# A state-space scan and its squared-ReLU network on one core: small products gathered in one region per block, other PSUM banks, DMA transposes, other weight packets

## The chip, the core and the metric

The kernel runs on one core of a Trainium2 chip. TensorE (PE) multiplies: a weight load puts a stationary block into its array, a matmul streams another operand through it, and the result lands in PSUM, which has eight banks of 512 fp32 columns on 128 partitions. VectorE (DVE) and ScalarE (ACT) read PSUM and work on SBUF; GpSimd (POOL) works on SBUF alone; SyncE (SP) and ACT issue DMAs. Each engine runs its own instructions in order and waits on semaphores for the others.

The metric is the device time in microseconds. Each time below is a median over executions; lower is better.

## The reference

A chunked scan (chunks of 32 tokens in the reference; the kernel is free to choose) for 4 batches, 8 heads, 768 tokens, head size 32 and state size 16, then a two-layer network on the 3072 tokens.

```python
L = exp(cum[i] - cum[j]) * causal            # decay between tokens of a chunk
y = einsum(C_i, B_j) * L @ x                 # within the chunk
y += einsum(C, state) * exp(cum)             # from the state before the chunk
state = exp(sum(la)) * state + sum_j B_j x_j * exp(cum_last - cum_j)
...
h = maximum(Y @ w_in, 0)                     # Y: 3072 x 256, w_in: 256 x 2048
out = (h * h) @ w_out                        # w_out: 2048 x 256
```

## The kernel before

**Units and blocks.** The 3072 tokens are 12 units of 256: unit k is (batch b, third j) in the order of `PAIRS`, all batches of the first third, then of the second, then of the last. A unit is two chunks of 128 tokens (`u` = 0, 1); its tokens are split in even and odd (`r`). The scan of unit k gives a 256 x 256 tile `T[k]`, and block k of the network takes it. The decay is folded in by products: C is multiplied by the running product P of `a`, x by its inverse, and the state by the product over a chunk (`Ptot`).

**A unit's steps** (functions of the same names):
- `ph_load`: three DMAs for C, B and x. `ph_prep` (POOL): scaled C into a zeroed tile `cz`, B cast to `Bb`, scaled x into `xs`.
- `ph_tr`: six PE transposes of 128x128 into PSUM, then one DVE copy to `bct`.
- `ph_u`: 16 matmuls (64x32 weights) for the new part of the state, then DVE: `z` = U + state, S = z times Ptot, twice in a row.
- `ph_mt`: 16 matmuls (32x64 weights) of C with B, over four banks. `ph_mask` (DVE): four times 512 columns times the causal mask, into `mts`.
- `ph_y`: up to 16 matmuls with 32x32 weights from the state and 32 from `mts` and `xs`; ACT copies the result to `T`.

**A block of the network** is 8 steps. Step (blk, fp): `mm1` has four matmuls of 128x128 weights and 256 columns into one bank and ACT's ReLU; `square` on DVE; `mm2` four more into a bank that is kept over the block. After the last, ACT copies it to `osb` and SP stores it. In a step only the four large matmuls of mm1 and of mm2, 0.44 us each, are on PE.

**Order.** It is written out by hand: `with tc.manual_schedule()` (line 329), the loads, the first two units complete, and then a loop over 96 steps: mm1 of step s, what `todo` holds for s, the square of s-1, mm2 of s-4. A unit's pieces stand at five different steps (lines 393 to 404), each between two fours of large matmuls. The PSUM pools give two banks to mm1, two to mm2, four to the pieces of the scan.

**Weights.** Five pairs of DMAs (`load_w`), on ACT's and SP's queue, bring them as fp32, w_in in columns and w_out in rows of 1 KB; `cast_w` makes them bf16, w_in on ACT and w_out on POOL, in five pieces.

Of the kernel before, what the change touches and what calls it, by code (L numbers as in the profile page):

```python
# [30 lines left out]
def kernel(  # L31
# [13 lines left out]

    nc = tc.nc
    NH, S, D, N = 8, 768, 32, 16
    NPAIR = 12
    LAG = 4
    LEAD = 12  # L50
# [6 lines left out]
    big = ctx.enter_context(tc.tile_pool(name="big", bufs=2))  # L57
# [5 lines left out]
    ps_h = ctx.enter_context(tc.tile_pool(name="ps_h", bufs=2, space=bass.MemoryType.PSUM))  # L63
    ps_o = ctx.enter_context(tc.tile_pool(name="ps_o", bufs=2, space=bass.MemoryType.PSUM))
    ps_s = ctx.enter_context(tc.tile_pool(name="ps_s", bufs=1, space=bass.MemoryType.PSUM))


    tok = 2 * np.arange(64)[None, :] + np.arange(2)[:, None]
    later = tok.reshape(-1)
    mask_np = np.zeros((128, 2, 128), np.float32)  # L70
    for u in range(2):
        for r in range(2):
            mask_np[64 * u:64 * u + 64, r, :] = (tok[r][:, None] <= later[None, :])
# [6 lines left out]
    cb_np = np.concatenate([np.eye(128, dtype=np.float32), mask_np.reshape(128, 256)],  # L80
                           axis=1).astype(ml_dtypes.bfloat16)
# [4 lines left out]
    cb = const.tile([128, 384], BF16, name="cb")  # L86
# [13 lines left out]
    cz = [const.tile([128, 2, 240], BF16, name=f"cz{i}") for i in range(3)]  # L100
# [6 lines left out]
    PAIRS = [(b, j) for j in range(3) for b in range(4)]  # L107


    loaded = {}  # L110

    def ph_load(k, order="CBx", eng=None):
        b, j = PAIRS[k]
        t = {}
        for what in order:
            src, w = {"B": (B, N), "C": (C, N), "x": (x, D)}[what]
            dst = nat.tile([128, NH, 2 * w], FP32, tag=f"{what}_nat", name=f"{what}_nat{k}")
            (eng or nc.sync).dma_start(  # L118
                out=dst, in_=_dap(src, (b * NH * S + j * 256) * w,
                                  [[2 * w, 128], [S * w, NH], [1, 2 * w]]))  # L120
            t[what] = dst
        loaded[k] = t

    def load_w(f0, f1, eng):
        eng.dma_start(  # L125
            out=w_in_f[:, :, f0 * 128:f1 * 128],
            in_=_dap(moe_w_in, f0 * 128, [[2048, 128], [128 * 2048, 2], [1, (f1 - f0) * 128]]))
        eng.dma_start(  # L128
            out=w_out_f[:, f0:f1, :],
            in_=moe_w_out[f0 * 128:f1 * 128, :].rearrange("(f p) d -> p f d", p=128))  # L130

    def cast_w(f0, f1):
        nc.scalar.copy(out=w_in_b[:, :, f0 * 128:f1 * 128], in_=w_in_f[:, :, f0 * 128:f1 * 128])  # L133
        nc.gpsimd.tensor_copy(out=w_out_b[:, f0:f1, :], in_=w_out_f[:, f0:f1, :])  # L134

# [3 lines left out]
    def prep_c(k, eng):  # L139
        b, j = PAIRS[k]  # L140
        czk = cz[k % 3]
        eng.tensor_tensor(  # L142
            out=_fap(czk, 0, [[240, 2], [32, 8], [1, 16]]),
            in0=_fap(loaded[k]["C"], 0, [[16, 2], [32, 8], [1, 16]]),
            in1=_fap(P_sb, b * 24 + j, [[96, 2], [3, 8], [0, 16]]), op=ALU.mult)
        live.setdefault(k, {})["cz"] = czk

    def prep_b(k, eng):
        Bb = prep.tile([128, 2, 128], BF16, tag="Bb", name=f"Bb{k}")
        for r in range(2):  # L150
            bo = _fap(Bb, r * 128, [[16, 2], [32, 4], [1, 16]])
            bi = _fap(loaded[k]["B"], r * 16, [[128, 2], [32, 4], [1, 16]])
            if eng is nc.scalar:
                eng.copy(out=bo, in_=bi)  # L154
            else:
                eng.tensor_copy(out=bo, in_=bi)  # L156
        live.setdefault(k, {})["Bb"] = Bb

    def prep_x(k, eng):
        b, j = PAIRS[k]  # L160
# [14 lines left out]
    def ph_tr(k):  # L175
        v = live[k]
        pool, tag = (ps_o, "ops") if k < 2 else (ps_s, "A")
        tr = pool.tile([128, 2, 3, 128], BF16, tag=tag, name=f"tr{k}",
                       padded_shape=[128, 2, 4, 128] if k < 2 else [128, 8, 4, 128])
        for r in range(2):  # L180
            nc.tensor.transpose(tr[:, r, 0, :], v["Bb"][:, r, :], eye_b)  # L181
            for g in range(2):
                nc.tensor.transpose(tr[:, r, 1 + g, :], v["cz"][:, r, 112 * g:112 * g + 128], eye_b)  # L183
        bct = big.tile([128, 2, 3, 128], BF16, tag="bct", name=f"bct{k}")
        nc.vector.tensor_copy(out=bct, in_=tr)  # L185
        v["bct"] = bct

    def ph_mt(k):
        v = live[k]
        bct = v["bct"]  # L190
        mt = ps_s.tile([128, 4, 2, 2, 128], FP32, tag="A", name=f"mt{k}")
        for u in range(2):
            for r in range(2):
                for q in range(4):
                    nc.tensor.matmul(  # L195
                        mt[64 * u:64 * u + 64, q, r, :, :],
# [4 lines left out]
        v["mt"] = mt  # L201
        v["mts"] = big.tile([128, 4, 2, 2, 128], BF16, tag="mts", name=f"mts{k}")

    def ph_mask(k, q):
        v = live[k]
        nc.vector.tensor_tensor(  # L206
            out=v["mts"][:, q], in0=v["mt"][:, q],
            in1=_fap(cb, 128, [[128, 2], [0, 2], [1, 128]]), op=ALU.mult)

    def ph_u(k):  # L210
        b, j = PAIRS[k]
        v = live[k]
        if k < 2:
            U = [ps_h.tile([128, 64], FP32, tag="hps", name=f"U{k}_{u}", padded_shape=[128, 512])
                 for u in range(2)]
        else:
            t = ps_s.tile([128, 4, 512], FP32, tag="A", name=f"U{k}")
            U = [t[:, u, 0:64] for u in range(2)]
        for r in range(2):
            for u in range(2):  # L220
                if j == 2 and u == 1:
                    continue
                for q in range(4):
                    nc.tensor.matmul(  # L224
                        U[u][32 * q:32 * q + 32, :],
                        v["Bb"][64 * u:64 * u + 64, r, 32 * q:32 * q + 32],
                        _fap(v["xs"][64 * u:64 * u + 64], r * 256 + q * 32, [[128, 2], [1, 32]]),
                        start=(r == 0), stop=(r == 1), skip_group_check=True,
                        tile_position=(64 * u, 32 * q))
        S_u = [state.get(b)]  # L230
        for u in range(2):
            if j == 2 and u == 1:
                break
            ptot = Ptot[:, u, b * 3 + j:b * 3 + j + 1]
            S_n = spool.tile([128, 64], BF16, tag=f"S{b}{u}", name=f"S{k}_{u}")
            if S_u[u] is None:
                nc.vector.tensor_scalar(out=S_n, in0=U[u], scalar1=ptot, scalar2=None, op0=ALU.mult)  # L237
            else:
                z = spool.tile([128, 64], FP32, tag="z", name=f"z{k}_{u}")
                nc.vector.tensor_tensor(out=z, in0=U[u], in1=S_u[u], op=ALU.add)  # L240
                nc.vector.tensor_scalar(out=S_n, in0=z, scalar1=ptot, scalar2=None, op0=ALU.mult)
            S_u.append(S_n)
        v["S"] = S_u
        state[b] = S_u[-1]

    T = {}

    def ph_y(k):
        b, j = PAIRS[k]
        v = live.pop(k)  # L250
        if k < 2:
            Y = [ps_h.tile([128, 2, 128], FP32, tag="hps", name=f"Y{k}_{u}", padded_shape=[128, 4, 128])
                 for u in range(2)]
        else:
            t = ps_s.tile([128, 4, 4, 128], FP32, tag="A", name=f"Y{k}")
            Y = [t[:, u, 0:2, :] for u in range(2)]
        first = {(u, q): True for u in range(2) for q in range(4)}
        for u in range(2):
            S_b = v["S"][u]
            if S_b is None:  # L260
                continue
            for g in range(2):
                for q in range(4):
                    nc.tensor.matmul(  # L264
                        Y[u][32 * q:32 * q + 32, g, :],
                        S_b[32 * q:32 * q + 32, g * 32:(g + 1) * 32],
                        _fap(v["bct"][32 * q:32 * q + 32], 128 + g * 128 + u * 64, [[384, 2], [1, 64]]),
                        start=first[(u, q)], stop=False, skip_group_check=True,
                        tile_position=(32 * q, 32 * q))
                    first[(u, q)] = False  # L270
        for g in range(2):
            for r in range(2):
                for u in range(2):
                    for q in range(4):
                        h = 4 * g + q
                        nc.tensor.matmul(  # L276
                            Y[u][32 * q:32 * q + 32, g, :],
                            v["xs"][64 * u:64 * u + 64, r, h * 32:h * 32 + 32],
                            v["mts"][64 * u:64 * u + 64, q, r, g, :],
                            start=first[(u, q)], stop=(g == 1 and r == 1), skip_group_check=True,  # L280
# [163 lines left out]
```

## Time and profile before

| | us |
|---|---|
| median of 3 runs (131.95 to 132.62) | 132.33 |
| span of the profiled execution | 129.5 |
| PE busy in it | 111.8 |
| DVE busy | 90.4 |
| ACT busy | 75.7 |
| POOL busy | 31.6 |

The profiled execution's span runs from its first to its last instruction; the time of a run lies 2.83 us above it. Granted TensorE clock: 0.997. A line of the chain of waits has the start, the length and what was on the path then. In a table of windows, each engine has its busy time and, in brackets, its instructions. In a line on groups "idle before" is the time its engine sat still just before, and the arrow names what ended it. L numbers are lines of the kernel.

### The profile page before, as it was taken

The page shows a single profiled execution, that of the slowest core. Times are in us where ns is not written, and L with a number is a line of the kernel's source. Part 1 is how long each engine was busy: PE and PEld are TensorE (multiplying, and loading weights), DVE is VectorE, ACT ScalarE, POOL GpSimd, SP SyncE. Part 2 cuts the span into 40 slices and gives each one's busy share as a digit, 9 for nine tenths or more (in the row PEclk, how much of TensorE's full clock was granted, in tenths as well). Part 3 has the DMA queues.
Part 4 walks back from the last instruction along what each step waited for, and adds up shares of the span by engine and source line. Part 5 has one row for each costly group of instructions (what it writes and reads, how often), then busy time and mean ns, then how long its engine had stood idle before and what let it go on. Part 6 is the DMA issues. An engine that isn't in the chain of part 4 may idle for free.

```text
span 129.5 us, 4148 instructions
## 1 busy us (share of the span) xinstructions
PE 111.8 (86%) x1740; PEld 87.8 (68%) x1740; DVE 90.4 (70%) x201; ACT 75.7 (58%) x134; POOL 31.6 (24%) x54
## 2 busy tenths in 40 slices
PE   0126648699999999999999999999999999999980
PEld 0013315557877787788778777887887787788860
DVE  0519592379899698795896995886977938744520
ACT  0413308867757657658467476576584675687740
POOL 4015236335907025060070240330330000000000
PEclk9999999999999999999999999999999999999998
DMA  4999999978391280650831903805602010020202
GB/s 95 257 165 262 294 175 269 318 148 154 96 200 21 88 161 6 137 106 5 177 69 47 196 10 96 149 3 135 116 0 89 3 68 18 0 86 0 81 0 81
DMA packets 43043, 14.18 MB, mean 110 GB/s; under 512 B 37840, under 2 KB 40720, under 8 KB 43024
## 3 DMA queue, kind: packets, MB, share of 16 engines
q1 hardware_dynamic: 42224, 13.21, 43.8%
q10 hardware_dynamic: 800, 0.71, 1.8%
q8 instruction: 13, 0.21, 0.7%
q14 instruction: 6, 0.05, 0.1%
HBM read 10.77 MB, written 3.15 MB: 107 GB/s over the span
## 4 chain that ended last, share of the span: by engine, by line
PE 76%; SPq 11%; DMA 8%; ACT 1%; issue 1%
PE ops L321 34%; PE hps L301 30%; SPq L118 8%; DMA w_in_f<-in_moe_w_in_dram 6%; PE mt L195 3%; PE Y L276 3%; PE Y L264 2%; DMA cf<-const_f 2%; SPq L125 2%; PE tr L183 2%; PE U L224 1%; SPq L128 1%; ACT w_in_b L133 1%; PE tr L181 1%; ACT osb L326 0%
## 5 line engine op out<-in xcount | busy, mean ns | idle before, releaser
L305 ACT ACTIVATE hb<-hps 128x512 bf16<-128x512 f32 x96 | 57.5, 599 | 32.2 <-PE hps L301 31.1
L301 PE MATMUL hps<-T,w_in_b 128*128 128x256 bf16 x384 | 58.5, 277 | 1.8 <-ACT w_in_b L133 1.4
L321 PE MATMUL ops<-w_out_b,h 128*128 128x256 bf16 x384 | 57.3, 273 | 0.0
L311 DVE TENSOR_TENSOR h<-hb 128x512 bf16<-128x512 bf16 x96 | 45.9, 500 | 9.4 <-ACT hb L305 9.4
L301 PEld LDWEIGHTS <-w_in_b 128*128 128x128 bf16 x384 | 38.0, 99 | 7.6 <-ACT w_in_b L133 1.9
L321 PEld LDWEIGHTS <-h 128*128 128x128 bf16 x384 | 34.7, 98 | 7.0 <-issue 2.0
L206 DVE TENSOR_TENSOR mts<-mt,cb 128x512 bf16<-128x512 f32 x48 | 31.5, 685 | 2.8 <-PE mt L195 2.7
L162 POOL TENSOR_TENSOR xs<-x_nat,Pinv 128x512 bf16<-128x512 f32 x12 | 13.5, 1126 | 15.0 <-DMA x_nat<-in_x_dram 11.7
L142 POOL TENSOR_TENSOR cz<-C_nat,P_sb 128x256 bf16<-128x256 f32 x10 | 6.8, 682 | 40.4 <-DMA C_nat<-in_C_dram 28.8
L185 DVE COPY bct<-tr 128x768 bf16<-128x768 bf16 x12 | 6.7, 556 | 13.4 <-PE tr L183 13.4
L326 ACT COPY osb<-ops 128x512 f32<-128x512 f32 x12 | 7.0, 580 | 1.6 <-PE ops L321 1.6
L276 PE MATMUL Y<-mts,xs 64*32 64x128 bf16 x384 | 6.2, 232 | 1.8 <-DVE mts L206 1.8
L181 PE MATMUL tr<-cb,Bb 128*128 128x128 bf16 x24 | 5.1, 232 | 3.0 <-ACT Bb L154 3.0
L290 ACT CAST T<-Y 128x512 bf16<-128x512 f32 x10 | 5.9, 586 | 1.3
L195 PE MATMUL mt<-bct 32*64 32x256 bf16 x192 | 5.7, 302 | 0.7 <-DVE bct L185 0.7
L156 POOL CAST Bb<-B_nat 128x128 bf16<-128x128 f32 x20 | 5.8, 319 | 1.8 <-DMA B_nat<-in_B_dram 1.7
L264 PE MATMUL Y<-bct,S 32*32 32x128 bf16 x160 | 4.6, 225 | 1.9 <-DVE S L237 1.9
L276 PEld LDWEIGHTS <-xs 64*32 64x32 bf16 x384 | 3.4, 95 | 3.8 <-issue 1.7
L183 PE MATMUL tr<-cb,cz 128*128 128x128 bf16 x48 | 5.9, 235 | 0.0
L134 POOL CAST w_out_b<-w_out_f 128x1024 bf16<-128x1024 f32 (+1 forms) x5 | 4.3, 868 | 6.0 <-DMA w_out_f<-in_moe_w_out_dram 6.0
L264 PEld LDWEIGHTS <-S 32*32 32x32 bf16 x160 | 2.3, 91 | 4.3 <-DVE S L237 2.2
L287 ACT CAST T<-Y 128x256 bf16<-128x256 f32 x4 | 1.3, 376 | 6.5 <-PE Y L276 6.5
(29 smaller groups left out, 37.8 us busy)
## 6 DMA issues: line engine op xcount, KB each, us to landing
x_nat<-in_x_dram SPq DMA_DIRECT2D x12, 256.0 KB, 4.2
out_dram<-osb SPq DMA_DIRECT2D x12, 256.0 KB, 2.2
C_nat<-in_C_dram SPq DMA_DIRECT2D x12, 128.0 KB, 3.5
B_nat<-in_B_dram SPq DMA_DIRECT2D x12, 128.0 KB, 4.1
w_in_f<-in_moe_w_in_dram SPq DMA_DIRECT2D x3, 512.0 KB, 5.8
w_out_f<-in_moe_w_out_dram SPq DMA_DIRECT2D x3, 512.0 KB, 7.1
w_in_f<-in_moe_w_in_dram ACTq DMA_DIRECT2D x1, 256.0 KB, 4.8
w_out_f<-in_moe_w_out_dram ACTq DMA_DIRECT2D x1, 256.0 KB, 5.2
```

The source lines that it names most:

```text
L118: (eng or nc.sync).dma_start(out=dst, in_=_dap(src, (b * NH * S + j * 256) * w, [[2 * w, 128], [S * w, NH], [1, 2 * w]]))
L162: eng.tensor_tensor(out=_fap(xs, 0, [[256, 2], [32, 8], [1, 32]]), in0=_fap(loaded[k]["x"], 0, [[32, 2], [64, 8], [1, 32]]), in1=_fap(Pinv ...
L183: nc.tensor.transpose(tr[:, r, 1 + g, :], v["cz"][:, r, 112 * g:112 * g + 128], eye_b)
L195: nc.tensor.matmul(mt[64 * u:64 * u + 64, q, r, :, :], bct[32 * q:32 * q + 32, r, 0, u * 64:u * 64 + 64], _fap(bct[32 * q:32 * q + 32], 12 ...
L206: nc.vector.tensor_tensor(out=v["mts"][:, q], in0=v["mt"][:, q], in1=_fap(cb, 128, [[128, 2], [0, 2], [1, 128]]), op=ALU.mult)
L264: nc.tensor.matmul(Y[u][32 * q:32 * q + 32, g, :], S_b[32 * q:32 * q + 32, g * 32:(g + 1) * 32], _fap(v["bct"][32 * q:32 * q + 32], 128 + ...
L276: nc.tensor.matmul(Y[u][32 * q:32 * q + 32, g, :], v["xs"][64 * u:64 * u + 64, r, h * 32:h * 32 + 32], v["mts"][64 * u:64 * u + 64, q, r, ...
L301: nc.tensor.matmul(hps[:, i, :], w_in_b[:, g, f * 128:(f + 1) * 128], T[blk][:, g].rearrange("p r u t -> p (r u t)"), start=(g == 0), stop ...
L305: nc.scalar.activation(out=hb, in_=hps, func=AF.Relu)
L311: nc.vector.tensor_tensor(out=h2, in0=hb, in1=hb, op=ALU.mult)
L321: nc.tensor.matmul(ops[blk][:, r, :], h2[:, i, r * 128:(r + 1) * 128], w_out_b[:, f, :], start=(f == 0 and r == 0), stop=(f == 15), skip_g ...
L326: nc.scalar.copy(out=osb, in_=ops.pop(blk).rearrange("p r d -> p (r d)"))
```

## The change

- The transposes of units 4 to 11 are DMA transposes on SP's queue, SBUF to SBUF. B and scaled C are for this put side by side in one tile `jt` per unit (three of them, zeroed once).
- All PSUM is one tile `pp` of eight banks: 0 to 3 for `ph_mt`, 4 to 6 in turn for everything else (`bank`, `two_banks`), 7 for mm2.
- The state is also kept as a 128x256 block-diagonal tile (`S_d`), so that Y from the state is two full-array matmuls a chunk. `ph_s` has z on DVE and the two scalings on POOL.
- Y of unit k, U of unit k+1 and the products of `ph_mt` of unit k+1 stand together, once a block (`ph_yu`, then `ph_mt`). U and Y share a bank: columns 256 to 319 and 0 to 255.
- The mask is applied to two banks at a time.
- w_out is read so that a partition gets 2 or 4 neighbouring rows (2 or 4 KB); the columns of w_in are taken in the matching order when they are cast. The casts are eight pieces, two before the loop.
- Only unit 0 is complete before the loop; unit 1 is made in the first eight steps. In a step, `todo` comes before mm1. B of unit 0 is loaded from ACT's queue, all weights from SP's; the loads of later units are issued ten steps earlier.

```diff
-    ps_h = ctx.enter_context(tc.tile_pool(name="ps_h", bufs=2, space=bass.MemoryType.PSUM))
-    ps_o = ctx.enter_context(tc.tile_pool(name="ps_o", bufs=2, space=bass.MemoryType.PSUM))
-    ps_s = ctx.enter_context(tc.tile_pool(name="ps_s", bufs=1, space=bass.MemoryType.PSUM))
+    psum = ctx.enter_context(tc.tile_pool(name="psum", bufs=1, space=bass.MemoryType.PSUM))
...
+    pp = psum.tile([128, 8, 512], FP32, name="pp")
+    turn = [4]
+    def bank():
+        h = turn[0]
+        turn[0] = 4 if h == 6 else h + 1
+        return h
+    def two_banks():
+        h = turn[0] if turn[0] < 6 else 4
+        turn[0] = 6 if h == 4 else 4
+        return h, h + 1
...
-    def cast_w(f0, f1):
-        nc.scalar.copy(out=w_in_b[:, :, f0 * 128:f1 * 128], in_=w_in_f[:, :, f0 * 128:f1 * 128])
-        nc.gpsimd.tensor_copy(out=w_out_b[:, f0:f1, :], in_=w_out_f[:, f0:f1, :])
+    def cast_w(fp):
+        f = 2 * fp
+        f0, f1 = next(x for x in BLOCKS if x[0] <= f < x[1])
+        nc.scalar.copy(out=_fap(w_in_b, f * 128, [[2048, 2], [128, 2], [1, 128]]),
+                       in_=_fap(w_in_f, f0 * 128 + f - f0, [[2048, 2], [1, 2], [f1 - f0, 128]]))
+        nc.gpsimd.tensor_copy(out=w_out_b[:, f:f + 2, :], in_=w_out_f[:, f:f + 2, :])
...
     def ph_tr(k):
+        if k >= NPE:
+            nc.sync.dma_start_transpose(out=bct.rearrange("p r w t -> p (r w) t"),
+                                        in_=jt[k % 3].rearrange("p r w t -> p (r w t)"))
+            return
...
+    def ph_mask(k, q0, q1):
+        nc.vector.tensor_tensor(
+            out=live[k]["mts"][:, q0:q1].rearrange("p q r g i -> p q (r g i)"), in0=pp[:, q0:q1, :],
+            in1=_fap(cb, 128, [[0, q1 - q0], [1, 512]]), op=ALU.mult)
+
+    def ph_yu(y=None, u=None, late=False):
+        h = two_banks()
...
+        def from_state():
+            for i in range(2):
+                S_i = live[y]["S"][i]
...
+                for g in range(2):
+                    mm(i, range(4), pp[:, h[i], g * 128:(g + 1) * 128], S_i[:, g * 128:(g + 1) * 128],
+                       _fap(live[y]["bct"], 128 + g * 128 + i * 64, [[384, 2], [1, 64]]), None)
...
+            T[y] = tpool.tile([128, 2, 2, 2, 64], BF16, tag="T", name=f"T{y}")
+            nc.scalar.copy(out=_fap(T[y], 0, [[64, 2], [128, 4], [1, 64]]),
+                           in_=_fap(pp, h[0] * 512, [[512, 2], [64, 4], [1, 64]]))
...
+    def ph_s(k, i):
+        U = pp[:, v["h"][i], 256:320]
...
+            nc.vector.tensor_tensor(out=z, in0=U, in1=prev, op=ALU.add)
+            nc.gpsimd.tensor_scalar(out=S_c, in0=z, scalar1=ptot, scalar2=None, op0=ALU.mult)
+        S_d = spool.tile([128, 256], BF16, tag=f"Sd{b}{i}", name=f"Sd{k}_{i}")
+        nc.gpsimd.tensor_tensor(
+            out=_fap(S_d, 0, [[128, 2], [32, 4], [1, 32]]), in0=_fap(S_c, 0, [[32, 2], [0, 4], [1, 32]]),
+            in1=_fap(cb, 640, [[0, 2], [1, 4], [0, 32]]), op=ALU.mult)
...
     def mm1(blk, fp):
-        hps = ps_h.tile([128, 2, 256], FP32, tag="hps", name=f"hps{blk}_{fp}")
+        h = bank()
...
     with tc.manual_schedule():
...
+        ph_load(0, "C")
+        ph_load(0, "B", nc.scalar)
+        ph_load(0, "x")
         nc.scalar.dma_start(out=cb, in_=cb_d.ap())
-        load_w(0, 2, nc.scalar)
+        load_w(0)
+        load_w(1)
         ph_load(1)
...
+        cast_w(0)
+        cast_w(1)
+        ph_yu(y=0, late=True)
...
+        for fp in range(2, 8):
+            at(fp - 2, cast_w, fp)
...
+        at(2, ph_tr, 1)
+        at(3, ph_yu, u=1)
+        at(3, ph_mt, 1)
...
+        at(7, ph_yu, y=1)
+        at(8, ph_tr, 2)
...
+        for k in range(2, NU):
+            s0 = 8 * k - 4
...
+            at(s0, ph_yu, y=k, u=k + 1)
+            at(s0, ph_mt, k + 1)
+            for i in range(2):
+                at(s0 + 1 + i, ph_s, k + 1, i)
+                at(s0 + 1 + i, ph_mask, k + 1, 2 * i, 2 * i + 2)
+        for k in range(2, NU):
+            if k >= 4:
+                at(8 * k - 34, ph_load, k)
+            at({2: 4, 3: 9, 4: 12}.get(k, 8 * k - 25), ph_prep, k)
+            if k >= 3:
+                at({3: 10, 4: 16}.get(k, 8 * k - 20), ph_tr, k)
         for s in range(len(steps) + LAG):
+            for fn, args, kw in todo.pop(s, []):
+                fn(*args, **kw)
             if s < len(steps):
                 mm1(*steps[s])
-            for fn, args in todo.pop(s, []):
-                fn(*args)
             if 1 <= s <= len(steps):
                 square(*steps[s - 1])
             if s >= LAG:
                 mm2(*steps[s - LAG])
```

## The prediction

> **What bounds the kernel now.** I read the page's busy shares first, then its slices, then the chain of waits, and last two stretches of that chain closely: the start and one block in the middle.
>
> ```profile
> PE 111.8 (86%) x1740; PEld 87.8 (68%) x1740; DVE 90.4 (70%) x201; ACT 75.7 (58%) x134; POOL 31.6 (24%) x54
> ...
> PE   0126648699999999999999999999999999999980
> ...
> DMA  4999999978391280650831903805602010020202
> ...
> PE 76%; SPq 11%; DMA 8%; ACT 1%; issue 1%
> ```
>
> There are two stages. In the first eight slices (to about 26 us) the DMA row is 9 and the PE row is not; after it PE is 9 to the end. The chain from 18 to 34 us shows where one hands over to the other:
>
> ```profile
> 18.81 7.32 DMA w_in_f<-in_moe_w_in_dram
> 26.13 0.02 issue
> 26.15 1.05 ACT w_in_b L133
> 27.21 0.05 issue
> 27.25 0.61 PE hps L301 x4
> ```
>
> So the last quarter of w_in lands at 26.13 us, is cast, and from 27.25 us PE never rests until 125.87 us. Then 3.6 us follow (the last copy and the last store) up to the span of 129.5 us. One block in the middle, in the chain from 60 to 78 us:
>
> ```profile
> 62.02 0.18 PE U L224 x16
> 62.20 0.54 PE ops L321 x4
> 62.75 0.44 PE hps L301 x4
> 63.18 0.40 PE mt L195 x16
> 63.58 0.54 PE ops L321 x4
> ...
> 67.18 0.33 PE Y L264 x16
> 67.51 0.35 PE Y L276 x32
> 67.86 0.54 PE ops L321 x4
> ```
>
> Four large matmuls take 0.44 us, but 0.54 after small products: coming back costs 0.10. A block is 16 such fours, 16 x 0.437 = 7.0 us, plus a unit: transposes 0.34, U 0.18, mt 0.40, Y 0.68 and three returns 0.30, together 1.90. The same transposes stand 8.90 us apart (60.81 and 69.71), which is the sum. Before 27.25 us PE had done six fours of mm1 and two of mm2 and the first pieces of unit 2, 4.2 us; so the loop behaves as if it had begun at 23.0 us and never stopped.
>
> The rate of the loads is in the table of windows (the last two columns are the DMA share and GB/s):
>
> ```profile
> 16.00:18.00 2.00, 0.81 (x10) 0.33 (x11) 1.86 (x6) 0.00 (x0) 0.00 (x0) 1.00 1.00 168
> 22.00:24.00 2.00, 1.35 (x8) 0.77 (x6) 1.08 (x3) 1.72 (x3) 0.00 (x0) 1.00 1.05 341
> ```
>
> The first is a unit's B, C and x in 128 and 256 byte pieces, the second is weights.
>
> **What the Trainium skill says.** "TensorEngine Tiling (Array Packing)", Key Properties: changing the tiling mode drains TensorE. The trace agrees (0.54 beside 0.44). "PSUM — Partial Sum Buffer", PSUM bank collisions raise a hardware error: two engines may not touch the same bank and 32 partitions at once, so PSUM must be guarded by bank and quadrant, reads included. No run here shows a collision, but the changed program's waits follow it, which matters below. "DMA: Bandwidth & Descriptors", Latency and other measured facts: a DMA transpose moves 261 GB/s; its Anatomy section gives about 2 us fixed. No trace here has one.
>
> **The change part by part.** Times are against the profiled execution; its median of runs, 132.33, lies 2.83 above its span, and I add that at the end.
>
> *The start.* In the program before, each cast of w_in waits for the DMA of its own columns. In the changed one, the wait lists of the built program make the first cast on ACT wait for all five blocks of w_in: the strided source view reaches over both halves of the tile. Behind that cast on ACT stand the second cast, the copy of T0, and every ReLU; mm1 needs T0. So nothing of the loop runs before the last w_in block lands. When? What precedes it is the same: a, constants, units 0 to 2, weights but the last w_out block, 5.5 MB. The queue was full in that time, so 26.1 is the base. cb grows by 65 KB (+0.2); 1.5 MB of w_out come in pieces of 2 or 4 KB instead of 1: at 341 GB/s they took 4.6 us, and I take a fifth off, 0.9 (ends: 0 and 2.6). B0 moves to ACT's queue, but shares the same engines: 0. Landing at about 25.3 us (23.5 to 26.4). Then two casts of 128x512, 0.62 each by the same form before (its source had no stride, so this is a floor), and T0 0.59 with wake-ups: mm1 begins at 27.2.
>
> *PE work after that.* The fours: 192 x 0.437 = 83.9. Unit 0 is done under the loads. Unit 1: transposes 0.34, U and mt with a return 0.6, Y 0.65: 1.6. Unit 2 0.94 (its Y is in the region), transposes of unit 3 0.34. A region: four full-array matmuls from the block-diagonal state at half the 0.109 of a 256-column one, 0.22; entry into tiles 0.12; Y 0.35; U 0.06 to 0.18; mt 0.28 to 0.40; one return 0.10: 1.25, or 1.1 where the first chunk has no state, 1.2 where U is halved. 2 x 1.1 + 3 x 1.25 + 4 x 1.2 + 0.8 for the last = 11.5. Together 14.4, where before it was 18.9 (ten units from 2 on). Gain 4.5, of which the DMA transposes give 8 x 0.34 = 2.7.
>
> *PE waiting on banks in the first blocks.* Large products now have three banks, of which U and Y take two. On ACT eight casts of 0.62 alternate with ReLUs of 0.60, 1.22 a step where PE needs 0.44 to 0.87. Counting from the landing: the third ReLU ends at 5.5, and U of unit 1 needs its bank; the sixth ends at 9.55, and Y of unit 1 needs its; T1 ends at 10.95, and the transposes of unit 2 need its. The region of unit 2 starts at 16.2, after 11.6 of PE work begun at 1.9: 2.7 lost. There DVE has mask, bct copy, square, mask in a row, and Y waits 0.75 for the second mask. Together 3.4 (1.5 to 5).
>
> *PE waiting on banks later.* Let the region start at 0. U ends at 0.81; the copy of T on ACT waits for it and holds both banks to 1.5. The program makes z (DVE) wait for that copy, then DVE's order is z of the first half (0.22), a mask of two banks, the square, z of the second half. A mask of 1024 columns: four of 512 took 2.47 in a row, so about 1.2. The square waits for a ReLU that ends at 2.3. This gives z at 1.78, mask at 3.0, square at 3.4, second z at 3.64. mm1 two steps after the region takes that bank; PE arrives at 2.95 and goes on at 3.7. 0.72 lost, five times (units 3 to 7): 3.6. Units 8 to 11 have no second half and lose nothing; mm1 one step after arrives at 2.08 for z at 1.78. In every second region the second bank was used by the mm1 just before, whose ReLU ends 0.25 after the region starts: 0.15 x 5 = 0.8. The single bank of mm2 costs nothing: its copy is over at 0.8, mm2 comes at 1.64.
>
> *DMA transposes.* 0.2 MB at 261 GB/s and 2 us is an estimate of 2.8 us by the skill. They stand on SP behind the store of the last block and before the next unit's loads, and have 8 steps, 7 us after the store; unit 4 has as much. So 0; each us over 7 would cost about 8. A floor below 0 is excluded: PE has lost that work already in the sum above.
>
> *Edits that cost nothing.* POOL takes Sc and Sd: by the nearest rows (0.32 for 128x128, 0.68 for 128x256) 2.0 a block beside 2.4 of preparation, in a block of 8 to 9; even doubled it is hidden. DVE loses the bct copies and the second scalings, worth nothing while PE is the bound. Preparation in two halves, earlier loads (units 4 on, ten steps) and casts of w_out are on queues with slack.
>
> *Sum.* 27.2 + 83.9 + 14.4 + 3.4 + 3.6 + 0.8 = 133.3, against 125.87; with 3.6 behind it a span of 136.9, and **139.7 us** as a time. The gain on PE is real (4.5), but the start gives back 4.2 and the waits on banks 7.8.
>
> **The rivals.** *PE stays fed* (faster): copies and z's are over before PE comes back, and inside a region no change of form drains. Then 7.8 and about 1.0 of the 14.4 go: span 128.1, **130.9 us**. For it: ACT 58% and DVE 70% busy look like slack. Against: averages; the waits come from order and position, not load. It decides once less than 1 us of idle PE is left after 27.2. *The cast holds nothing back*, the last block landing early enough or its wait not binding: mm1 then starts on the first weights as before, but the fourth mm1 pair still needs late blocks; six fours done at 27, 126.7 for PE's end, **133.1 us**. Against: the list of waits, and the queue full up to 26 us. *Transposes come late*: at 9 us each, 2 us lost eight times, about **156 us**. For it: 128-row reordering in 2-byte elements, never seen in this trace; against: the skill's rate.
>
> **How the numbers follow.** Forecast 0.70 (135 to 143), cast not binding 0.10, PE fed 0.13, late transposes 0.07. Range 132.0 to 144.0 leaves out PE fed and late transposes. A change under 0.5% could not be told from none in this kernel (runs 131.95 to 132.62). Faster 0.11 (PE fed, less its upper part), same 0.04, slower 0.85.
>
> **What would show it.** Right: the first large matmul near 27 us, released by ACT behind the w_in DMA; blocks in the middle 8.9 to 9.1 us apart while units 3 to 7 are made and 8.1 to 8.3 after; PE idle about 0.7 before the mm1 two steps after a region, released by DVE z; PE's transposes down to 24. Wrong: mm1 well before 25 us, PE 9 in all later slices with no z wait, or mt waiting for a DMA.

## The result and the profile after

The kernel after takes 140.03 us (median of 4 runs, 139.26 to 140.42) where the kernel before takes 132.14 (4 runs, 131.47 to 132.62) on the same chip: 1.061 times as long, 95% interval 1.056 to 1.067. The forecast was 139.7. The profiled span is 137.5 us; 136.9 was forecast. For the last two experiments below only the ratio is given: most of their executions (12 and 19 of 22) ran at a lower granted clock, and the ratio leaves those out.

The page of the kernel after: the row of busy times, PE's and the DMA engines' slices, and the shares of the chain of waits.

```profile
PE 108.0 (79%) x1572; PEld 89.3 (65%) x1572; DVE 84.0 (61%) x158; ACT 78.7 (57%) x133; POOL 55.3 (40%) x104
...
PE   0164000569999898998998989999999999999990
...
DMA  5999999996001679539929599187902802010101
...
PE 61%; DVE 9%; ACT 9%; SPq 9%; DMA 7%; issue 2%; ACTq 1%; DVEq 0%
```

PE is busy for 3.8 us less than before (108.0 against 111.8), as the change meant, and the span is 8.0 us longer. PE's slices say where: 000 in the fifth to seventh slice (13.8 to 24 us), where the kernel before had 648, and then 8s among the 9s up to 82 us, where it had only 9s. ACT and DVE, 1% and nothing shown on the chain before, have 9% each.

The start, from the chain of waits between 20 and 50 us (start, length, what was on the path):

```profile
19.07 4.58 DMA w_in_f<-in_moe_w_in_dram
...
24.26 0.64 ACT w_in_b L148
24.90 0.49 ACT T L271
25.39 0.04 issue
25.43 1.03 PE pp L308 x4
26.46 0.02 issue
26.48 0.60 ACT hb L312
27.08 1.00 ACT w_in_b L148
28.07 0.50 ACT hb L312
28.57 0.99 ACT w_in_b L148
```

The last block of w_in lands at 23.65 (19.07 + 4.58). Only then does ACT cast the first piece; T0 and the first large matmul follow. After that the chain alternates between casts and ReLUs on ACT and leaves PE out.

What PE waited for, in the whole program (total us, times, longest us):

```profile
PE pp L308 <- ACT T L271: 12.4, 1, 12.4
...
PE pp L308 <- DVE z L292: 2.3, 5, 0.5
```

These two answer to the prediction: one wait of 12.4 us until the first casts are over, and five for z. Two regions in the middle, from PE's timeline (start, length, line, operation; in brackets the idle time before and what ended it):

```profile
60.25 0.69 PE L232 MATMUL pp<-bct,Sd 128*128 128x128 bf16 x4
60.86 0.42 PE L232 MATMUL pp<-mts,xs 64*32 64x128 bf16 x32
...
61.72 0.61 PE L308 MATMUL pp<-T,w_in_b 128*128 128x256 bf16 x4
...
64.09 0.60 PE L308 MATMUL pp<-T,w_in_b 128*128 128x256 bf16 x4 [0.45 <-DVE z L292]
...
69.33 0.39 PE L232 MATMUL pp<-bct,Sd 128*128 128x128 bf16 x4
...
70.51 0.61 PE L308 MATMUL pp<-T,w_in_b 128*128 128x256 bf16 x4
```

The region from 69.33 is over in 1.18 us, the one from 60.25 in 1.47: its four matmuls from the state stretch over 0.69 in place of 0.39. The second pair needs the bank that the mm1 just before has used, and waits for its ReLU. Two steps after a region, mm1 stands for z: the mm2 before it began at 63.04 and takes 0.44, so 0.61 us is lost up to 64.09. A block that begins with a long region and has the z wait takes 9.08 us (60.25 to 69.33), one that begins with a short region 8.78 (69.33 to 78.11).

### The profile page after: what moved, and what is told of

The parts are those of the page before. It is cut to its first block, busy times and chain, and to the rows that moved or that the text cites. A ratio compares the mean times of both kernels' runs of the same rounds, so it can differ in the third digit from the quotient of the medians.

```text
span 137.5 us, 3855 instructions
## 1 busy us (share of the span) xinstructions
PE 108.0 (79%) x1572; PEld 89.3 (65%) x1572; DVE 84.0 (61%) x158; ACT 78.7 (57%) x133; POOL 55.3 (40%) x104
## 4 chain that ended last, share of the span: by engine, by line
PE 61%; DVE 9%; ACT 9%; SPq 9%; DMA 7%; issue 2%; ACTq 1%; DVEq 0%
PE pp L308 28%; PE pp L326 25%; SPq L130 7%; PE pp L232 6%; DVE mts L219 5%; DMA cb<-const_b 4%; ACT hb L312 3%; DMA w_in_f<-in_moe_w_in_dram 3%; ACT T L271 3%; ACT w_in_b L148 2%; DVE h L318 2%; PE pp L210 2%; DVE z L292 1%; ACT osb L332 1%; SPq L138 1%
## 5 line engine op out<-in xcount | busy, mean ns | idle before, releaser
L312 ACT ACTIVATE hb<-pp 128x512 bf16<-128x512 f32 x96 | 57.4, 598 | 29.7 <-PE pp L308 29.6
L308 PE MATMUL pp<-T,w_in_b 128*128 128x256 bf16 x384 | 60.0, 282 | 14.7 <-ACT T L271 12.4
L326 PE MATMUL pp<-w_out_b,h 128*128 128x256 bf16 x384 | 57.6, 275 | 0.3 <-ACT osb L332 0.3
L219 DVE TENSOR_TENSOR mts<-pp,cb 128x1024 bf16<-128x1024 f32 (+1 forms) x26 | 29.2, 1131 | 0.8 <-PE pp L210 0.8
L293 POOL TENSOR_SCALAR Sc<-z,Ptot 128x64 f32<-128x64 f32 x16 | 7.1, 443 | 35.5 <-DVE z L292 35.5
L148 ACT CAST w_in_b<-w_in_f 128x512 bf16<-128x512 f32 x8 | 7.8, 990 | 15.4 <-DMA w_in_f<-in_moe_w_in_dram 15.4
L295 POOL TENSOR_TENSOR Sd<-Sc,cb 128x256 bf16<-128x256 f32 x20 | 12.2, 612 | 10.2 <-DVE Sc L289 8.9
L157 POOL TENSOR_TENSOR jt<-C_nat,P_sb 128x128 bf16<-128x128 f32 x20 | 10.7, 554 | 0.0
L271 ACT CAST T<-pp 128x512 bf16<-128x512 f32 x12 | 7.0, 584 | 2.9 <-PE pp L232 2.6
L169 POOL CAST jt<-B_nat 128x128 bf16<-128x128 f32 x22 | 7.2, 353 | 0.0
```

The source lines that it names most:

```text
L148: nc.scalar.copy(out=_fap(w_in_b, f * 128, [[2048, 2], [128, 2], [1, 128]]), in_=_fap(w_in_f, f0 * 128 + f - f0, [[2048, 2], [1, 2], [f1 - ...
L157: eng.tensor_tensor(out=_fap(jt[k % 3], 128 + 144 * g, [[384, 2], [32, 4], [1, 16]]), in0=_fap(loaded[k]["C"], 128 * g, [[16, 2], [32, 4], ...
L219: nc.vector.tensor_tensor(out=live[k]["mts"][:, q0:q1].rearrange("p q r g i -> p q (r g i)"), in0=pp[:, q0:q1, :], in1=_fap(cb, 128, [[0, ...
L271: nc.scalar.copy(out=_fap(T[y], 0, [[64, 2], [128, 4], [1, 64]]), in_=_fap(pp, h[0] * 512, [[512, 2], [64, 4], [1, 64]]))
L295: nc.gpsimd.tensor_tensor(out=_fap(S_d, 0, [[128, 2], [32, 4], [1, 32]]), in0=_fap(S_c, 0, [[32, 2], [0, 4], [1, 32]]), in1=_fap(cb, 640, ...
L308: nc.tensor.matmul(pp[:, h, i * 256:(i + 1) * 256], w_in_b[:, g, f * 128:(f + 1) * 128], T[blk][:, g].rearrange("p r u t -> p (r u t)"), s ...
```

## The experiments

All numbers are ratios to the kernel before on the same chip, since the kernel before takes 131.15 to 132.14 us on the chips used; 0.01 is 1.3 us. The kernel after stands at 1.061.

| run | median us | ratio (95%) | profiled span |
|---|---|---|---|
| e1 own wait | 132.62 | 1.010 (1.004 to 1.017) | 130.8 |
| e2 weights as before | 133.1 | 1.014 (1.007 to 1.020) | 131.3 |
| e3 z before masks | 137.44 | 1.047 (1.039 to 1.056) | 135.0 |
| e4 PE transposes | 143.15 | 1.091 (1.083 to 1.100) | 141.2 |
| e5 own wait and z first | 130.98 | 0.992 (0.986 to 0.998) | 128.5 |
| e6 and another start order | 128.9 | 0.979 (0.973 to 0.985) | 126.9 |
| e7 all blocks wait, no stride | 138.29 | 1.048 (1.041 to 1.056) | 136.6 |
| e8 state product in tiles | 140.11 | 1.062 (1.056 to 1.069) | 138.8 |
| e9 PE busy while waiting | 140.12 | 1.069 (1.062 to 1.076) | 138.0 |
| e10 start order 2 | 129.73 | 0.989 (0.983 to 0.994) | 127.6 |
| e11 last weights ahead of x | | 0.987 (0.984 to 0.991) | 127.6 |
| e12 and contiguous casts | | 0.985 (0.980 to 0.991) | |

### The wait of the first cast

e1 gives each block of w_in a staging tile of its own, so that a cast depends on its own block. Nothing else is changed.

```diff
-    w_in_f = stage.tile([128, 2, 2048], FP32, name="w_in_f")
+    w_in_f = [stage.tile([128, 2, (f1 - f0) * 128], FP32, name=f"w_in_f{f0}") for f0, f1 in BLOCKS]
```

> The changed kernel with one staging tile for each of the five blocks of w_in, so that a cast waits for its own block alone; the strided cast and all DMAs stay. Theory A (the start is lost in the first cast's wait for all blocks): the first large matmul near 18 us instead of 25.4; then ACT stops at the cast of the seventh piece, which stands ahead of the fifth ReLU, until the last block lands near 23.7 us; the transposes of unit 2 near 29 us instead of 37.2; 131 to 134 us in all. Rival B (the blocks land too late in any case, so the wait takes nothing away that is not taken again): 138 to 140 us.

From 1.061 to 1.010: the wait is worth 6.7 us, most of the loss. The first large matmul is at 13.70 us, earlier than expected, but then PE stands 3.2 us, to 18.76, for the transposes of unit 1: they wait for B of unit 1 on POOL, which stands behind a w_out cast that begins when its block has landed, at 16.86. What ended last in its place is in the chain of e1 between 12 and 38 us:

```profile
19.91 6.07 DMA w_out_f<-in_moe_w_out_dram
25.98 0.05 issue
26.03 0.62 POOL w_out_b L150
26.65 0.74 POOL Sd L295
...
30.00 0.52 PE pp L199 x6
```

POOL stands at the cast of a w_out block that lands at 25.98, and behind it on POOL stands the preparation of unit 2, whose transposes PE waits for until 30.00.

e2 undoes the packets instead: w_out in rows of 1 KB, w_in columns in their own order, so the casts read without a stride, and each can wait for its own columns.

```diff
-            in_=moe_w_out[f0 * 128:f1 * 128, :].rearrange("(p f) d -> p f d", p=128))
+            in_=moe_w_out[f0 * 128:f1 * 128, :].rearrange("(f p) d -> p f d", p=128))
...
-        nc.scalar.copy(out=_fap(w_in_b, f * 128, [[2048, 2], [128, 2], [1, 128]]),
-                       in_=_fap(w_in_f, f0 * 128 + f - f0, [[2048, 2], [1, 2], [f1 - f0, 128]]))
+        nc.scalar.copy(out=w_in_b[:, :, f * 128:(f + 2) * 128], in_=w_in_f[:, :, f * 128:(f + 2) * 128])
```

> The changed kernel with the weights read and cast as before (w_out in rows of 1 KB, w_in cast without a stride), which also gives each cast its own wait. Theory A: as in the run with own staging tiles, and 6 casts of 0.62 instead of 1.10 us: 130 to 133 us, the last w_in block landing within 1 us of 23.7. Rival B (the larger packets bring the weights earlier and are worth more than the stride costs): last w_in block near 25 us, slower than the run with own staging tiles by 1 us or more.

It can't be told from e1 (intervals 1.007 to 1.020 and 1.004 to 1.017). So once the wait is gone, packets and length of the casts together change nothing that can be measured; as e2 changes both at once, two small effects that cancel are not excluded. It also corrects the reason that the prediction gave for the wait, a view that reaches over both halves of the tile: the view of e2 reaches over both halves too, and its casts wait for their own blocks (at 9.15, 15.49, 18.34 and 24.88 us). The wait comes with the strided view; which property of it is the cause was not isolated.

### The stride of the casts

ACT's casts of w_in in the groups by form of the kernel after (busy us, mean ns of one | idle before):

```profile
L148 ACT CAST w_in_b<-w_in_f 128x512 bf16<-128x512 f32 x8 | 7.8, 990 | 15.4 <-DMA w_in_f<-in_moe_w_in_dram 15.4
```

The same group of e2:

```profile
L148 ACT CAST w_in_b<-w_in_f 128x512 bf16<-128x512 f32 x8 | 4.9, 615 | 4.2 <-DMA w_in_f<-in_moe_w_in_dram 4.2
```

The mean hides two kinds: in the timeline the two pieces from the small blocks (every second element) take about 0.6 us and the six from the large ones (every fourth) 1.10 to 1.12. To see what that costs while the wait is still there, e7 keeps the wait and takes the stride away: it is e2 with one column of the last w_in block copied on ACT ahead of the first cast.

```diff
+        last = const.tile([128, 1], FP32, name="last")
+        nc.scalar.copy(out=last, in_=w_in_f[:, 1, 2047:2048])
```

> The kernel after with contiguous w_in casts and w_out rows of 1 KB again, but with a one-column ScalarE copy of the last w_in block ahead of the first cast, so that all casts still begin only when the last block has landed. Theory A (the stride made six casts 1.10 us long in place of 0.62, six times 0.48 = 2.9 us on ScalarE while TensorE waits for it): 137 to 137.7 us. Rival B (what bounds the first blocks after the landing is something else, VectorE's masks or the state copies, and the length of the casts is hidden): 139.5 to 140.5 us.

1.048 lies between the two theories, 0.013 or 1.7 us below the kernel after. In its profile the last block lands at 24.61, 0.96 later than in the kernel after's. The region of unit 2, from the timeline of e7:

```profile
40.80 0.28 PE L231 MATMUL pp<-bct,Sd 128*128 128x128 bf16 x2
...
42.07 0.41 PE L231 MATMUL pp<-mts,xs 64*32 64x128 bf16 x30 [0.84 <-DVE mts L218]
```

It begins at 40.80, 16.1 us after the first cast began (24.73). In the kernel after this took 18.6 (from 23.72 to 42.31), and in e3, e4, e8 and e9, which have the stride too, 17.8 to 18.5. The nearest to e7 are e3 and e8, with 17.8 and 17.9: in these three PE's slow first matmuls (below) end at most 4.7 us after they began, in the kernel after 8.9. So the 2.9 us on ACT (six times 0.48) move PE by about 1.7, and the other 0.7 of the kernel after goes with the slow matmuls. Inside the region, Y now stands 0.84 us for DVE's mask, and the chain of e7 there runs over DVE's masks and squares: part of the gain is taken by the next engine.

### z behind the masks

e3 puts both z of a unit ahead of both masks on DVE.

```diff
-                at(s0 + 1 + i, ph_s, k + 1, i)
+                at(s0 + 1, ph_s, k + 1, i)
+            for i in range(2):
                 at(s0 + 1 + i, ph_mask, k + 1, 2 * i, 2 * i + 2)
```

> The changed kernel with both halves of ph_s ahead of both masks in every region from unit 3 on. Theory A (PE waits for the second z behind a mask and a square on DVE, 0.55 to 0.6 us a region, five regions): no idle PE at the mm1 two steps after a region, 2.7 us less, 137.3 us. Rival C (DVE has no slack there: the wait moves to the masks, the squares or to POOL's scaling between the two z's): 139.5 us or more.

1.047: 0.014 or 1.9 us less. What PE waits for in e3:

```profile
PE pp L232 <- POOL xs L174: 1.0, 1, 1.0
...
PE pp L326 <- DVE h L318: 0.6, 4, 0.2
```

The five waits for z are gone, 0.6 us each. Four waits for a square, behind the moved masks, take part of it back: from the start of unit 2's region to PE's end e3 takes 90.3 us (41.03 to 131.34), the kernel after 91.5, so the order is worth 1.1 us there. The rest of the 1.9 lies ahead of that region, where the edit doesn't reach, and is a difference between two executions: the last w_in block landed 0.5 us earlier, and PE's slow first matmuls ended sooner. The wait of 1.0 for POOL, of the first Y of unit 1 at 34.48, lies there too; e8, with z in the old order, has it with 0.95.

e5 is e1 and e3 together.

> One staging tile for each block of w_in, so that a cast waits for its own block alone, and both state sums (z) ahead of both mask multiplications on VectorE. Theory A (the two waits lie at different places, the first block's and the later regions', so what they are worth adds): the earlier runs gave 7.4 and 2.6 us for them one by one, so 140.0 - 7.4 - 2.6 = 130.0 us, some 1% below the kernel before. Rival B (with the casts early, VectorE's masks in the first blocks or the loads end last, and the z order is worth nothing): 132 to 133 us. Rival C (the masks that now come later hold TensorE more once it is no longer delayed): above 133 us.

0.992. From e1 that is 2.4 us, from e3 7.3: the two waits add up, as they lie at different places. Without them the change is a gain of 0.8%.

### The DMA transposes and the block-diagonal state

e4 has PE make all transposes, four steps later than the DMA did (`NPE = 12`, and `ph_tr` of unit k at step 8k-16).

> The changed kernel with all transposes on PE as in the first four units, four steps later than the DMA transposes stood. Theory A (a DMA transpose lands in 4.2 us under 7 of cover and costs nothing, so the PE time is a pure gain): eight times 0.34 us more, 142.7 us. Rival D (the DMA transposes give their gain back through the queue of SP or the loads): 140 us or less.

The span is 3.7 us longer, by the ratio 4.0, not 2.7. Six transposes are 0.34 us on PE, eight units 2.7. The rest is in the regions. e4's timeline:

```profile
61.09 0.68 PE L232 MATMUL pp<-bct,Sd 128*128 128x128 bf16 x4
...
70.51 0.69 PE L232 MATMUL pp<-bct,Sd 128*128 128x128 bf16 x4
...
79.93 0.68 PE L232 MATMUL pp<-bct,Sd 128*128 128x128 bf16 x4
```

Now every region but the last is of the long form, where in the kernel after every second one is. The transposes take a turn of the three banks, which shifts the rotation so that a region always meets the bank of the mm1 just before. Three more long regions at 0.30 us and one wait of 0.25 in the region of unit 3 (at 52.02 us) are 1.15. In the kernel after the DMA transposes themselves are never waited for (the transposes as SP issues them; ns min/median/max, first and last start; then us from issue to landing):

```profile
L192 SPq DMA_TRANSPOSE bct<-jt x8: 1259/1314/2477, 47.1 to 105.0; - x8
...
DMA to landing us min/median/max: 3.6/4.2/4.6
```

e8 computes Y from the state in sixteen 32x32 tiles again, out of the diagonal blocks of the same tile.

```diff
-                    mm(i, range(4), pp[:, h[i], g * 128:(g + 1) * 128], S_i[:, g * 128:(g + 1) * 128],
-                       _fap(live[y]["bct"], 128 + g * 128 + i * 64, [[384, 2], [1, 64]]), None)
+                    for q in range(4):
+                        s = slice(32 * q, 32 * q + 32)
+                        mm(i, [q], pp[s, h[i], g * 128:(g + 1) * 128], S_i[s, g * 128 + 32 * q:g * 128 + 32 * q + 32],
+                           _fap(live[y]["bct"][s], 128 + g * 128 + i * 64, [[384, 2], [1, 64]]), (32 * q, 32 * q))
```

> The kernel after with the four full-array matmuls of Y from the block-diagonal state replaced by sixteen 32x32 ones that read the diagonal blocks of the same tile. Theory A (four full matmuls and the change of tile mode cost about what sixteen small ones did; the gain of the small products came from the transposes and from having one region): within 0.7 us of the kernel after, 139.3 to 140.7 us. Rival B (the block-diagonal form is what made the region shorter): at least 0.15 us for each of 11 regions more, above 141.6 us.

1.062 against 1.061: no difference that can be measured. The blocks have one: from the end of one region to the end of the next short one 8.79 us in the kernel after (61.72 to 70.51) and 8.89 in e8 (62.59 to 71.48), so 0.1 us for such a region. Where the region waits for the ReLU anyway, it is hidden. Rival B's price of 0.15 us in each of 11 regions is excluded.

### PE's slow first matmuls

In the kernel after, fours of large matmuls between 25.4 and 34.5 us take 0.85 us or more, later 0.44, while the granted clock reads 1.00 in both windows. The Trainium skill, "TensorE: Matmul & The Clock Gate", Part 1, states that the array falls to half rate when it has been idle for some 3.4 us and comes back after about as long of sustained work; PE had stood for 12.4. The prediction didn't consider it. Nor is it new: the first four fours of the kernel before, from 20.11 us, take 3.24. e9 lets PE work in that time, with 85 matmuls whose results nobody uses.

```diff
+        for _ in range(85):
+            nc.tensor.matmul(pp[:, 7, 0:256], eye_b, cb[:, 128:384], start=True, stop=True,
+                             skip_group_check=True)
```

> The kernel after with 85 extra matmuls (128x128 by 128x256, into bank 7, results unused) ahead of the first block, which keep TensorE working through the 12 us in which it waited for the first cast. Theory A (the fours of 0.85 to 1.03 us in the first 9 us of the blocks come of TensorE having stood still, but lie under ScalarE's casts and ReLUs, which took 1.5 us a piece there): the fours take 0.44 from the start, and the time stays within 0.7 us of the kernel after, 139.3 to 140.7 us. Rival B (the slow fours are on the path): about 8 fours with 0.42 too much, 3.4 us less, 136.0 to 137.5 us. Rival C (the slowness has nothing to do with standing still): the fours stay at 0.85.

PE's timeline in e9:

```profile
26.24 1.03 PE L308 MATMUL pp<-T,w_in_b 128*128 128x256 bf16 x8 [1.81 <-ACT T L271]
...
27.45 0.60 PE L308 MATMUL pp<-T,w_in_b 128*128 128x256 bf16 x4
29.25 0.21 PE L232 MATMUL pp<-xs,jt 64*32 64x64 bf16 x4 [1.21 <-ACT hb L312]
30.73 0.28 PE L232 MATMUL pp<-xs,jt 64*32 64x64 bf16 x12 [1.27 <-ACT hb L312]
30.95 0.65 PE L210 MATMUL pp<-bct 32*64 32x256 bf16 x16
31.53 1.89 PE L308 MATMUL pp<-T,w_in_b 128*128 128x256 bf16 x8
```

The first three fours are fast (eight matmuls in 1.03 where the kernel after takes 1.87), so rival C falls. The extra matmuls show the change of rate themselves: windows of half a us count 4 or 5 of them up to 17.0 us and 7 from 17.5 on, so full rate came after some 4 us of work without a pause, near what the skill states. They bring nothing: PE then stands twice for a ReLU, 1.21 and 1.27 us, and is slow again at 31.53, against what theory A expected. Before that it had worked 0.2 of 2.7 us, a shorter stand than the skill's 3.4. This time the clock shows it, in the slices of e9's profile:

```profile
PEclk9999999995999999999999999999999999999998
```

The 5 is the slice from 31 to 34.5 us. The kernel after has 9 in all slices, and slow fours all the same: the row does not show the half rate of the first matmuls.

The time is that of the kernel after or a little above it (140.12 us; the intervals of the ratios overlap): the first three fours lay under ACT's casts and ReLUs, and rival B is wrong for them. For the fours behind these e9 decides nothing, as they stayed slow, and there the chain of the kernel after is PE itself:

```profile
30.99 1.82 PE pp L308 x8
32.80 0.85 PE pp L326 x4
33.66 0.85 PE pp L308 x4
```

In e3 and e8 these fours were fast (in e3 the eight matmuls from 30.15 us take 1.05), and unit 2's region began 17.8 and 17.9 us after the first cast, against 18.6 in the kernel after and 18.5 in e4, where they were slow. So they cost about 0.7 us, an estimate from four executions; PE at once stood 0.95 us for POOL in e3 and e8. Why full rate came sooner there was not found.

### Towards a version that beats both

e6 is e5 with the start in another order: the w_out casts of the last two pieces on POOL in the steps just ahead of their use, the last two w_in casts one step later, and unit 2's preparation ahead of the last w_out cast.

The new `cast_o` has the POOL line of `cast_w` alone.

```diff
-            at(fp - 2, cast_w, fp)
+            at(fp - 2 if fp < 6 else fp - 1, cast_w, fp)
...
+        at(6, cast_o, 6)
+        at(7, cast_o, 7)
...
-            at({2: 4, 3: 9, 4: 12}.get(k, 8 * k - 25), ph_prep, k)
+            at({2: 3, 3: 9, 4: 12}.get(k, 8 * k - 25), ph_prep, k)
```

> As the kernel with both waits taken away, and the start reordered besides: the GpSimd casts of w_out's last two pieces stand in the steps where the pieces are first needed, ScalarE's last two w_in casts one step later, and the third unit's preparation ahead of the last w_out cast on GpSimd. Theory A (GpSimd stood at the last w_out cast for a block that landed at 26.0 us, ahead of the preparation that the third unit's first transposes wait for, 3.9 us in two waits): 2 to 3 us less than without the reordering, 127 to 128.5 us. Rival B (the landing of the weights or VectorE's masks bound the first block anyway): within 0.7 us of the kernel without it.

0.979: 1.7 us less than e5, a little under what was expected, and 2.1% faster than the kernel before (1.5 to 2.7). It is the best version found. Slow fours lie on its chain too, from 21.63 to 25.14 us; what full rate would bring there was not tried. Its chain between 6 and 36 us has the next cause of the same kind:

```profile
10.09 6.34 DMA w_out_f<-in_moe_w_out_dram
16.44 0.05 issue
16.49 1.36 POOL w_out_b L147 x2
17.86 0.49 POOL jt L174 x2
18.34 0.05 issue
18.39 0.82 PE pp L204 x6
```

POOL waits for w_out again, ahead of unit 1's B. e10 puts these casts behind it, to steps 1 to 4.

> As the kernel with own waits, z first and the start reordered, with GpSimd's casts of w_out's pieces 3 to 6 also put behind the preparation of the second unit, to the steps just ahead of their use. Theory A (TensorE stood 2.9 us for the second unit's first tiles, which stood behind a cast on GpSimd for a block that landed at 16.4 us): up to 2.9 us less, of which the slow fours and ScalarE's casts take some back: 126.5 to 128 us. Rival B (ScalarE's casts or the landing of the w_in blocks end last as soon as this wait is gone): within 0.7 us of 128.9.

0.989, 1.3 us more than e6, where rival B said within 0.7; the intervals overlap by a little. The cause that rival B named is there: PE's transposes are made at 15.42 in place of 18.39, and the casts of the late w_in blocks end last in their place. The chain of e10 there is SP's queue:

```profile
15.92 3.76 SPq L130
19.68 0.04 issue
19.72 5.11 DMA w_in_f<-in_moe_w_in_dram
24.83 0.02 issue
24.86 0.04 ACT w_in_b L152
```

The issue of x for unit 2 (L130) holds the queue for 3.76 us ahead of the last w_in block. (The issue of 3.48 us before it, which the next expectation counts as one of x, is that of B.) e11 issues that block and its w_out first.

> As the kernel with the second start order, with the last blocks of w_in and w_out issued ahead of the third unit's C, B and x on SP. Theory A (what ended last in that kernel was SP: two issues of x that took 3.5 and 3.8 us stood ahead of the last w_in block, which landed at 24.8, and ScalarE's cast of piece 7 waited 2.0 us for it): 1 to 2.5 us less, 127.2 to 128.8 us. Rival B (ScalarE's casts of 1.1 us between the ReLUs, or the third unit's loads that now come later, end last): 129.2 us or more.

0.987, as e10: unit 2's x now lands at 24.96 and POOL's scaling of it ends last, so rival B. e12 adds contiguous casts and 1 KB rows to e11.

> As the kernel with the last weights ahead, with contiguous casts of w_in and w_out rows of 1 KB again. Theory A (with neither the landing nor GpSimd ending last, ScalarE does, which does a cast of 1.1 us and a ReLU of 0.6 for each piece of the first block): six casts 0.48 us shorter, of which 1 to 2.5 us are seen, 125.5 to 127.5 us. Rival B (packets of 1 KB bring the weights later, or TensorE's slow fours of 0.85 us bind instead): within 0.7 us of the kernel without it.

0.985, which can't be told from e11: theory A is excluded, and rival B's number held. What ends last in e12 was not shown. None of the three is better than e6. In e10 and e11 it is each time another load that ends last; whether an order of loads exists that keeps all of this was not tried.

## Why the prediction was right

The forecast (0.70) was the right case and the time within 0.3 us; its sum hit partly because two errors cancelled. By its own steps, with L for the landing of the last w_in block:

| step | forecast | measured in the profile after |
|---|---|---|
| landing L | 25.3 | 23.65 |
| mm1 begins | L + 1.9 | L + 1.8 (25.43) |
| region of unit 2 begins | L + 16.2 | L + 18.7 (42.31) |
| from there to PE's end | 91.8 | 91.5 (133.76) |
| of it: z waits | 5 x 0.72 | 5 x 0.6 |
| of it: ReLU wait in every second region | 5 x 0.15 | 0.30 each |
| PE's end | 133.3 | 133.76 |

- **The first cast waits for all blocks: right**, and shown by e1. It is 6.7 of the 7.9 us.
- **The landing was 1.65 us too late** in the forecast, at the edge of its range. The term of the packets is not seen: with the same loads the block landed between 23.16 (e3) and 24.70 (e8), and e7, with the old packets, lies in that spread at 24.61, 1.5 ahead of the 26.13 before. The block was issued at the same time as before (19.07 and 18.81), but in the kernel after the weight blocks ahead of it had all been issued by 11.9, where before one was issued only at 16.84; that this brings it forward was not tested.
- **The casts: the mis-sized term.** "0.62 each by the same form before (its source had no stride, so this is a floor)" was used as the value. Two casts came out near it and six at 1.10. At the third ReLU, with two strided casts on the path, ACT was at L + 6.4 where the forecast had 5.5, and the region of unit 2 slid by 2.5. e7, with casts of 0.62, has that region at L + 16.2. About 1.7 of the 2.5 is the stride, by e3 and e8.
- **PE's half rate at the start: missing** from the forecast. For the first three fours e9 shows that it cost nothing; the later ones are the other 0.7 or so of the 2.5.
- **The z wait: right** in place, cause and number; 0.12 us too large each. z came 1.91 us after the start of a long region and 1.61 after that of a short one (forecast 1.78), mm1 went on after 3.84 and 3.54 (3.7). e3 shows the cause, and that taking the wait away is worth less than the wait, since a square then waits.
- **The ReLU wait** was put at half its size. The other terms of a region were a little too large (1.18 for 1.25, 1.11 for 1.2, 0.67 for 0.8), so the sum over the regions held.
- **The block's period: right** within 0.2. From 51 us on 8.7 to 9.1 us up to 87 us, 8.1 and 8.4 after it.
- **DMA transposes: right that they cost nothing**, though the estimate of 2.8 us by the Trainium skill ("DMA: Bandwidth & Descriptors", Latency and other measured facts, and Anatomy) was low: 4.2. The Anatomy section gives its 2 us for DMAs issued from GpSimd; these are issued from SP. From issue to the first product that reads the tile there were 7.4 to 8.6 us, but for unit 4 only 5.1 (47.10 to 52.22), where the forecast said as much as for the others: there the margin was small. Their worth was 2.7 by the forecast, and 3.7 to 4.0 by e4, with the bank rotation that the forecast left out.
- **The edits at nothing: right** for POOL, whose Sc took 0.44 for 0.32; it was 40% busy and late only in the start, where PE came to it sooner (e1, e3, e8).

Of the rivals, "The cast holds nothing back" put the kernel at 133.1 us with PE's end at 126.7, and e1, which takes that wait away, has 132.62 and 127.13: the picture was sound, though e1 begins its large matmuls earlier and then waits for POOL. "PE stays fed" put 130.9, and e5 has 130.98, but that is chance: the rival kept the late start and had no waits on banks, e5 has the early start and some of these waits.

## What to carry to other kernels

A saving on the busiest engine is kept only if its inputs and its buffers are ready sooner too: here 3.8 us of PE work saved became a loss of 7.9 through one wait that covered five loads instead of one, and through z standing behind a mask that had no hurry. Look at what a load's first reader really waits for, above all when it reads one big tile with a stride, and give each piece a tile of its own. In an in-order queue, put what frees a buffer ahead of what only has to be ready a block later.

## What the runs showed of the hardware

- ACT's cast of 128x512 fp32 took 1.10 us where it read every fourth element and about 0.6 where it read every second or all.
- PE ran its first large matmuls at half rate (0.85 us for four in place of 0.44): for 8.9 us of interrupted work in the kernel after, for at most 4.7 in e3 and e8, and for some 4 us of work without a pause in e9. In e9 the half rate came back after 2.7 us in which PE had worked 0.2. There the granted clock read 0.50; at the start of the kernel after it read 1.00.
- An issue of x on SP (128 partitions, 256 KB in small pieces) held the queue for up to 4.4 us in the start (e11), where the very first one took 0.58 (e6): what stands behind it on the queue is late by as much.
- A DMA transpose of 128x768 bf16 from SBUF to SBUF took 3.6 to 4.6 us from issue to landing, and held SP's queue for 1.3 to 2.5.
